# Unit 1's turns in the matmul banks, later clears on GpSimd, and the g product between the first turns of the keys

## The chip, the core and the metric

The kernel runs on one core of one Trainium2 chip. The metric is the device time of one execution, in microseconds (us). A core has a matrix engine, TensorE (PE in the profile, with its weight loads as PEld), three engines for everything else, VectorE (DVE), ScalarE (ACT) and GpSimd (POOL), and SyncE (SP), which issues DMAs only. GpSimd issues DMAs too: all loads from memory that change fp32 to fp16 on the way are issued by it, in the order of its program. Each engine works through its own instructions in order and waits where an operand is not ready.

TensorE writes to PSUM, a memory of eight banks that VectorE and ScalarE can read[...]. All other tiles are in SBUF.

## What is computed

Attention in chunks of 32 rows, then a layer norm, a two-layer network with a ReLU, and a residual:

```
for c in range(nc):                       # 24 chunks of 32 rows
    q_c = q[:, :, c_start:c_end]
    k_full = concat([mem_k, k[:, :, c_start - 16 : c_end + 8]], axis=2)   # 8 mem rows
    v_full = concat([mem_v, v[:, :, c_start - 16 : c_end + 8]], axis=2)
    a = softmax(scale * q_c @ k_full.T)
    attn[:, :, c_start:c_end] = a @ v_full
x  = attn as [4, 768, 512]                # 8 heads of 64
xn = (x - mean(x)) / sqrt(var(x) + 1e-6) * g_ln
out = x + max(xn @ w_ch1, 0) @ w_ch2      # 512 -> 2048 -> 512
```

There are 4 batches of 8 heads and 768 rows.

## The kernel before

Every engine's order is written out by hand: what the program calls first, the engine does first. A batch's 768 rows are 12 groups of 64 (two chunks); two groups make a tile of 128 rows, three tiles a unit. There are eight units, two per batch. The part that concerns us is the first two units, which are batch 0 and are interleaved by hand (lines 471 to 616); from unit 1's second half on, a plan of steps takes over (lines 619 to 717).

The steps of one tile, by function and line:

- `load_kq`, `load_v_group` (L105, L114): GpSimd loads keys, queries and values. The first 64 rows of `k16` and 48 of `q16` come first (`CUT`), in two halves of four heads; the rest later.
- `turn_kq` (L185): TensorE turns keys or queries of two heads (a "pair" j of four), 16 matmuls against the identity, into a PSUM bank. `keep_k` (L197) copies turned keys to `KT`, on VectorE unless told otherwise; `keep_q` (L210) copies turned queries to `QZ`, ScalarE or VectorE. `QZ` holds each query block beside a block of zeros, so that one matmul serves two heads; `clear_q` (L444) writes these zeros.
- `keep_mem` (L143) copies the 8 mem rows of the values into rows 96 to 103 of every group of `V`.
- `scores` (L293): 8 matmuls into an `att` buffer of two banks, then two exp on ScalarE into `AT`. `values` (L314): 16 matmuls into the next `att` buffer. `norm` (L326): VectorE divides (`xs`, L330), takes the mean (L336) and writes `xn` (L339), scaled by `g_row`, which is g_ln spread over all partitions by a product of a row of ones with g_ln (L492). `xs` is the last to read the `att` buffer.
- `turn_x` (L354): TensorE turns `xn` with four matmuls (L362), and ScalarE copies the result to `xT` (L367).
- `up` (L380): four matmuls (L387) into an `mm` bank and a ReLU on ScalarE (L393) or VectorE (L395). `hc` counts 16 blocks of 128 columns; block `hc` needs chunk `hc // 4` of `w1c`. `down` (L399) is the second layer.
- `stay_busy(n)` (L372): n matmuls on a tile of zeros whose result nobody reads. They fill time on TensorE.

PSUM has two `att` buffers of two banks and four `mm` banks, handed out in turn by `slot(kind)` (L86). A new user of a buffer waits for the last reader of the old one.

In the opening, TensorE runs eight fillers, the mem keys, and the g product; then the first turns of keys and queries for pairs 0 and 1, three fillers, keys of pairs 2 and 3, four fillers, and queries of pairs 2 and 3, which go into the banks that held the keys of pairs 0 and 1. GpSimd meanwhile issues loads (lines 509 to 526): values of groups 3 to 5, the first chunk of `w1c`, the remaining rows of keys and queries, the second chunk, values of groups 6 and 7, and so on to `w2c`. Tiles 0 to 2 need only groups 0 to 5; the second half of the queries and keys (groups 6 to 11) is turned in two `kq_block`s (L583), just ahead of which VectorE clears the later rows of `QZ` and copies the later mem rows (L579 to L581).

Of the kernel before, what the change touches and what calls it, by code (L numbers as in the profile page):

```python
# [15 lines left out]
def kernel(  # L16
# [12 lines left out]
    nc = tc.nc  # L29
# [3 lines left out]
    NG = 12  # L33
# [15 lines left out]
    g_row = sb.tile([128, 512], FP32, name="g_row")  # L49
    g_one = sb.tile([1, 512], FP32, name="g_one")  # L50
    ones32 = sb.tile([1, 128], FP32, name="ones32")
# [13 lines left out]
    QZ = [sb.tile([128, NG, 4, 2, 64], FP16, name=f"QZ{i}") for i in range(2)]  # L65
# [16 lines left out]
    att = [ps.tile([128, 2, 512], FP32, name=f"att{i}") for i in range(2)]  # L82
    mm = [ps.tile([128, 512], FP32, name=f"mm{i}") for i in range(4)]
    turn = {"att": 0, "mm": 0}

    def slot(kind):  # L86
        lst = {"att": att, "mm": mm}[kind]
        turn[kind] = (turn[kind] + 1) % len(lst)
        return lst[turn[kind]]

    def dram(t, offset, pattern):
        return bass.AP(tensor=t.tensor, offset=offset, ap=[list(p) for p in pattern])

    def free(ap, off, pattern, parts=None):

        p = list(ap.ap[0]) if parts is None else [ap.ap[0][0], parts]
        return bass.AP(tensor=ap.tensor, offset=ap.offset + off, ap=[p] + [list(x) for x in pattern])

    def as16(t):
        return t.bitcast(FP16)  # L100
# [4 lines left out]
    def load_kq(b, which, lo=0, hi=96, h0=0, h1=H):  # L105

        dst, src = ((k16, k), (q16, q))[which]
        nc.gpsimd.dma_start(
            out=dst[lo:hi, h0:h1, :, :],
            in_=dram(src, (b * H + h0) * HS + 512 * lo,  # L110
                     [[512, hi - lo], [HS, h1 - h0], [1, 512]]),
        )

    def load_v_group(b, g):  # L114

        lo, hi = max(64 * g - 16, 0), min(64 * g + 80, S)
        r = 16 + lo - 64 * g
        nc.gpsimd.dma_start(  # L118
            out=V[b % 2][r : r + hi - lo, g, :, 0:64],
            in_=dram(v, b * H * HS + lo * D, [[64, hi - lo], [HS, H], [1, 64]]),  # L120
        )
# [18 lines left out]
                        ap=[list(src.ap[0]), [0, NG], [1, H * HD]]),  # L140
        )

    def keep_mem(b, g0, g1):  # L143

        src = memv16[:, b, :, 0:64]
        nc.vector.tensor_copy(
            out=V[b % 2][96:104, g0:g1, :, 0:64],
            in_=bass.AP(tensor=src.tensor, offset=src.offset,
                        ap=[list(src.ap[0]), [0, g1 - g0], [HD, H], [1, 64]]),
        )  # L150

    def load_w1(c):
        nc.gpsimd.dma_start(
            out=w1c[c], in_=dram(moe_w_ch1, 512 * c, [[FF, 128], [128 * FF, 4], [1, 512]])
        )
# [8 lines left out]
    def mem_keys():  # L164

        pv = slot("mm")
        for i in range(2):
            for par in range(2):
                nc.tensor.matmul(
                    out=pv[64 * par : 64 * par + 64, 64 * i : 64 * i + 64],  # L170
                    lhsT=memk16[:, i, :],
                    rhs=free(identity, 8 * par, [[16, 8], [1, 8]]),
                    start=True, stop=True, tile_position=(0, 64 * par),
                )
        nc.vector.tensor_copy(out=memKT.rearrange("p j m -> p (j m)"), in_=pv[:, 0:128])

    def mem_cols(b):
        src = memKT[:, 4 * b : 4 * b + 4, :]
        nc.vector.tensor_copy(
            out=free(KT[b % 2], 96, [[KW, 4], [4 * KW, NG], [1, 8]]),  # L180
            in_=bass.AP(tensor=src.tensor, offset=src.offset,
                        ap=[list(src.ap[0]), [8, 4], [0, NG], [1, 8]]),
        )

    def turn_kq(pv, src, j, n):  # L185

        for r in range(8):
            for par in range(2):
                nc.tensor.matmul(  # L189
                    out=pv[64 * par : 64 * par + 64, n * r : n * r + n],  # L190
                    lhsT=src[0:n, 2 * j + par, r, :],
                    rhs=identity[0:n, 0:n],
                    is_transpose=True, start=True, stop=True,
                    tile_position=(0, 64 * par),
                )
# [158 lines left out]
    def turn_x(u, i, t, kind="att"):  # L354
        if kind == "dma":
            nc.sync.dma_start_transpose(
                out=xT[u % 2][:, :, 128 * i : 128 * i + 128], in_=xn[t % 3]
            )
            return
        pv = as16(slot("att")[:, 0, :]) if kind == "att" else as16(slot("mm")[:, :])  # L360
        for dt in range(4):
            nc.tensor.matmul(  # L362
                out=pv[:, 128 * dt : 128 * dt + 128],
                lhsT=xn[t % 3][:, 128 * dt : 128 * dt + 128], rhs=identity,
                is_transpose=True, start=True, stop=True,
            )
        nc.scalar.copy(  # L367
            out=xT[u % 2][:, :, 128 * i : 128 * i + 128],
            in_=free(pv, 0, [[128, 4], [1, 128]]),
        )  # L370

    def stay_busy(n, p=None):  # L372

        p = slot("mm") if p is None else p
        for _ in range(n):
            nc.tensor.matmul(out=p, lhsT=busy[:, 0:128], rhs=busy, start=True, stop=True)  # L376
# [59 lines left out]
    def clear_k(i):  # L436
        end = 4 * KW * NG
        nc.vector.memset(free(KT[i], 0, [[KW, 4], [1, 16]]), 0.0)
        nc.vector.memset(free(KT[i], 88, [[KW, 4 * NG], [1, 8]]), 0.0)
        nc.vector.memset(free(KT[i], 104, [[KW, 4 * NG], [1, 8]]), 0.0)  # L440
        nc.vector.memset(free(KT[i], end - 4 * KW + 80, [[KW, 4], [1, 8]]), 0.0)
        nc.vector.memset(KT[i][:, end : end + 32], 0.0)

    def clear_q(i, par, g0=0, g1=NG):  # L444

        nc.vector.memset(QZ[i][64 - 64 * par : 128 - 64 * par, g0:g1, :, par, :], 0.0)

    TWO_ONES = (2.0 ** -7) * (1 + 15 * 2.0 ** -13)

    def clear_v(i, eng, between=lambda: None, end=HD // 2):  # L450

        eng.memset(V[i][0:32, 0, :, 0:64], 0.0)
        eng.memset(V[i][64:96, NG - 1, :, 0:64], 0.0)
        eng.memset(V[i].bitcast(FP32)[:, :, :, 32:end], TWO_ONES)
        between()
        for c, g, rows in ((0, 0, slice(0, 32)), (1, NG - 1, slice(64, 96))):
            eng.tensor_copy(
                out=free(V[i][rows, g, 0, 64:65], 0, [[HD, H]]),
                in_=free(counts[rows, c : c + 1], 0, [[0, H]]),
            )  # L460
# [24 lines left out]
    nc.scalar.copy(out=memk16, in_=memk32)  # L485
    nc.scalar.copy(out=QZ[0][0:64, 0:6, :, 1, :], in_=free(busy[0:64, :], 0, [[0, 6], [0, 4], [1, 64]]))
    nc.scalar.copy(out=memv16[:, 0, :, 0:64], in_=memv32.rearrange("p (h d) -> p h d", h=H))
    stay_busy(8)
    clear_v(0, nc.vector, lambda: (clear_q(0, 0, 0, 6), clear_k(0)), 33)
    mem_keys()  # L490
    spare = att[turn["att"]]
    nc.tensor.matmul(out=spare[:, 1, :], lhsT=ones32, rhs=g_one, start=True, stop=True)  # L492
    nc.scalar.copy(out=g_row, in_=spare[:, 1, :])
    spare = spare[:, 0, :]
    mem_cols(0)
    for g in range(3):
        load_v_group(0, g)
# [14 lines left out]
    for which in range(2):  # L512
        load_kq(0, which, CUT[which], 96)
    load_w1(1)
    for g in range(6, 8):
        load_v_group(0, g)
    load_w1(2)
# [3 lines left out]
    for c in range(4):  # L521
        load_w2(c)
    nc.gpsimd.dma_start(
        out=memv16[:, 1:B, :, 0:64],
        in_=dram(mem_v, H * 512, [[64, 8], [512, (B - 1) * H], [1, 64]]),
    )

    vec, act = nc.vector.tensor_copy, nc.scalar.copy
    banks = [slot("mm")[:, :] for j in range(4)]
    first_k = [as16(p) for p in banks]  # L530
    first = slot("att")
    first_q = [as16(first[:, i, :]) for i in range(2)] + first_k[0:2]
    for j in range(2):
        turn_kq(first_k[j], k16, j, CUT[0])
    for j in range(2):
        turn_kq(first_q[j], q16, j, CUT[1])
    for j in range(2):
        keep_k(first_k[j], 0, j, CUT[0], 0, 7)
        for par in range(2):
            keep_q(act, first_q[j], 0, j, par, CUT[1], 0, 6)  # L540
    stay_busy(3, spare)
    for j in range(2, 4):
        turn_kq(first_k[j], k16, j, CUT[0])
    for j in range(2, 4):
        keep_k(first_k[j], 0, j, CUT[0], 0, 7, act if j == 2 else vec)
    stay_busy(4, spare)
    for j in range(2, 4):
        turn_kq(first_q[j], q16, j, CUT[1])
    for g0, g1 in ((0, 2), (2, 6)):
        for j in range(2, 4):  # L550
            for par in range(2):
                keep_q(act if j == 2 else vec, first_q[j], 0, j, par, CUT[1], g0, g1)
    keep_mem(0, 0, 6)
    scores(0, 0)
    scores(0, 1)
    stay_busy(3)
# [19 lines left out]
    turn_x(0, 2, 2)  # L576
    for hc in range(4):
        up(0, 3, hc, 2)
    for par in range(2):  # L579
        clear_q(0, par, 6, NG)  # L580
    keep_mem(0, 6, NG)  # L581
    stay_busy(2)
    for j in (0, 2):  # L583
        kq_block(0, j, 6, NG, "mm", vec if j else act)
        keep_rest()
# [11 lines left out]
    norm(4, 4)  # L597
    up(0, 3, 11)
    scores(0, 5)
    turn_x(1, 0, 3)  # L600
    for hc in range(4):
        up(1, 1, hc)
    values(0, 5)
    norm(5, 5)
    turn_x(1, 1, 4)
    for hc in range(4, 8):
        up(1, 1, hc)
    for hc in range(8):
        up(1, 2, hc, 1)
    for hc in range(8, 12):  # L610
        up(1, 2, hc)
    turn_x(1, 2, 5)
    for hc in range(12, 16):
        up(0, 3, hc)
    for hc in range(12):
# [4 lines left out]
    for u, tiles in list(enumerate(units))[1:]:  # L620
# [86 lines left out]
        for step in range(12 if u == 1 else 0, last + 1):  # L707
            if step < 16:
                up(u, n, step)
            else:  # L710
                i, part = divmod(step - 16, 4)
# [36 lines left out]
```

## Time and profile before

| | |
|---|---|
| median of 6 runs | 227.16 us (225.70 to 228.32) |
| the profiled execution | 225.70 us, of which the span from first to last instruction is 224.0 us |
| TensorE busy | 214.2 us, 96% of the span |
| TensorE's weight loads | 134.3 us, 60% |
| VectorE | 120.2 us, 54% |
| GpSimd | 105.3 us, 47% |
| ScalarE | 103.3 us, 46% |
| mean granted TensorE clock | 0.976 |

All durations come from the one profiled execution; it is the fastest of the six runs shown. The profile's page cuts the span into 40 slices of 5.6 us. A row of the timeline gives start, duration, engine, line, operation, what it writes and reads, how many instructions are merged, and in square brackets how long the engine was idle before it and what ended that. The four loads of `w1c` (512 KB each, counted as written) took 7.9 to 13.8 us from issue to landing, a group of `V` (96 KB) typically 5.8 us; all sixteen DMA engines were busy from 6 us to about 50 us.

### The profile page before, as it was taken

To read this page: it belongs to the slowest core of one execution; us is meant where nothing else is said; L and a number is where in the kernel's file an instruction comes from. 1 tells how busy PE (TensorE), PEld (TensorE's weight loads), DVE (VectorE), ACT (ScalarE), POOL (GpSimd) and SP (SyncE) were. 2 spreads that over 40 slices of the span, in tenths; PEclk is the share of its full clock that TensorE was granted. 3 is DMA by queue.
4 is the path that set the end of the run, shared out by engine and by line. 5 is a ranking of instruction groups with operands and counts; after the bars stand their busy time and mean duration, and the time that the engine had idled before them with its cause. 6 is when DMAs were issued, how large, how long until landed. Compare 5 with 4: busy or idle time off the path is not lost.

```text
span 224.0 us, 5194 instructions
## 1 busy us (share of the span) xinstructions
PE 214.2 (96%) x2071; PEld 134.3 (60%) x2071; DVE 120.2 (54%) x285; ACT 103.3 (46%) x216; POOL 105.3 (47%) x185
## 2 busy tenths in 40 slices
PE   7999986999999989999999999999999999999994
PEld 2566765986555557644775467546764576457553
DVE  5457768647763853951537446723375436634222
ACT  6567565457656467620275146501654055503200
POOL 7993554202899962996201599815229100210000
PEclk9769999699999999999999999999999999999999
DMA  5999999990299999997611399998655300421012
GB/s 87 162 151 194 181 192 214 203 169 3 41 160 178 179 187 190 97 152 200 108 26 40 83 188 159 141 152 147 115 146 142 120 0 4 94 70 47 3 47 94
DMA packets 87610, 27.25 MB, mean 122 GB/s; under 512 B 78289, under 2 KB 84081, under 8 KB 87538
## 3 DMA queue, kind: packets, MB, share of 16 engines
q0 software_dynamic: 62128, 14.38, 74.8%
q1 hardware_dynamic: 25458, 12.54, 25.0%
q8 instruction: 16, 0.26, 0.5%
q14 instruction: 8, 0.07, 0.1%
HBM read 28.84 MB, written 6.29 MB: 157 GB/s over the span
## 4 chain that ended last, share of the span: by engine, by line
PE 90%; DVE 7%; issue 1%; ACT 1%; DVEq 0%
PE mm L387 36%; PE mm L404 35%; PE att L299 4%; PE att L319 3%; PE mm L376 3%; PE att L189 2%; PE mm L422 2%; DVE KT L204 1%; PE mm L189 1%; DVE xs L330 1%; DVE xn L339 1%; PE att L376 1%; PE att L362 1%; ACT xT L367 1%; DVE rT L395 1%
## 5 line engine op out<-in xcount | busy, mean ns | idle before, releaser
L387 PE MATMUL mm<-xT,w1c 128*128 128x384 f16 (+2 forms) x624 | 91.3, 301 | 2.6 <-ACT xT L367 2.0
L404 PE MATMUL mm<-w2c,rT 128*128 128x512 f16 x338 | 76.3, 379 | 0.0
L387 PEld LDWEIGHTS <-w1c 128*128 128x128 f16 x624 | 61.8, 116 | 23.9 <-issue 3.1
L393 ACT ACTIVATE rT<-mm 128x384 f16<-128x384 f32 (+2 forms) x68 | 30.6, 454 | 71.4 <-PE mm L387 49.2
L404 PEld LDWEIGHTS <-rT 128*128 128x128 f16 x338 | 32.5, 98 | 36.9
L395 DVE TENSOR_SCALAR rT<-mm 128x384 f16<-128x384 f32 (+2 forms) x60 | 32.1, 540 | 36.4 <-PE mm L387 36.4
L411 DVE SCALAR_TENSOR_TENSOR osb<-mm,rstd,xs 128x512 f32<-128x512 f32 x23 | 17.3, 750 | 41.5 <-PE mm L404 31.1
L306 ACT ACTIVATE AT<-att,band 104x512 f16<-104x512 f32 x48 | 30.1, 685 | 11.8 <-PE att L299 11.6
L348 POOL TENSOR_SCALAR veps<-squares 128x1 f32<-128x1 f32 x24 | 4.7, 194 | 53.1 <-ACT junk L345 51.7
L118 POOL DMA_DIRECT2D V<-in_v_dram x24 | 18.8, 788 | 5.7 <-DVE rT L395 3.1
L345 ACT ACTIVATE junk<-xs,nmean 128x512 f16<-128x512 f32 x24 | 17.3, 720 | 7.3 <-DVE nmean L336 4.4
L339 DVE SCALAR_TENSOR_TENSOR xn<-xs,nmean,g_row 128x512 f16<-128x512 f32 x24 | 18.6, 776 | 0.8
L330 DVE SCALAR_TENSOR_TENSOR xs<-att,rec 128x512 f32<-128x512 f32 x24 | 16.6, 692 | 0.8
L299 PE MATMUL att<-QZ,KT 128*128 128x128 f16 x192 | 15.5, 226 | 1.1 <-DVE QZ L214 1.1
L287 POOL COPY QZ<-kraw 64x768 f16<-64x768 f16 x16 | 14.1, 884 | 4.5 <-DMA kraw<-qraw 4.0
L299 PEld LDWEIGHTS <-KT 128*128 128x128 f16 x192 | 13.2, 101 | 4.5 <-issue 1.3
L352 POOL TENSOR_TENSOR rstd<-veps,mhalf 128x1 f32<-128x1 f32 x24 | 13.6, 568 | 2.0
L279 POOL COPY KT<-KT 128x128 f16<-128x128 f16 (+4 forms) x16 | 4.2, 291 | 17.3 <-DMA KT<-kraw 17.2
L124 POOL DMA_DIRECT2D V<-in_v_dram x16 | 12.0, 771 | 0.5 <-PE mm L387 0.4
L319 PEld LDWEIGHTS <-AT 104*64 104x64 f16 x384 | 7.6, 111 | 6.4 <-issue 1.9
L252 POOL DMA_DIRECT2D kraw<-in_k_dram x12 | 11.2, 929 | 0.2 <-issue 0.2
L252 POOL DMA_DIRECT2D qraw<-in_q_dram x12 | 11.2, 933 | 0.0
(83 smaller groups left out, 158.2 us busy)
## 6 DMA issues: line engine op xcount, KB each, us to landing
out_dram<-osb SPq DMA_DIRECT2D x23, 256.0 KB, 2.4
V<-in_v_dram POOLq DMA_DIRECT2D x36, 96.0 KB, 5.8
w1c<-in_moe_w_ch_dram POOLq DMA_DIRECT2D x4, 512.0 KB, 10.6
w2c<-in_moe_w_ch_dram POOLq DMA_DIRECT2D x4, 512.0 KB, 11.8
kraw<-in_k_dram POOLq DMA_DIRECT2D x12, 128.0 KB, 5.9
qraw<-in_q_dram POOLq DMA_DIRECT2D x12, 128.0 KB, 5.9
qraw<-in_q_dram POOLq DMA_DIRECT2D x3, 384.0 KB, 14.6
kraw<-in_k_dram POOLq DMA_DIRECT2D x3, 256.0 KB, 4.4
```

What stands on the lines that cost most here:

```text
L118: nc.gpsimd.dma_start(out=V[b % 2][r : r + hi - lo, g, :, 0:64], in_=dram(v, b * H * HS + lo * D, [[64, hi - lo], [HS, H], [1, 64]]),)
L252: nc.gpsimd.dma_start(out=free(dst, 512 * t, [[64, H], [1, 64]]), in_=dram(src, b * H * HS + 128 * t * D, [[D, 128], [HS, H], [1, 64]]),)
L299: nc.tensor.matmul(out=p[:, gg, 128 * j : 128 * j + 128], lhsT=KT[b % 2][:, (4 * g + j) * KW : (4 * g + j) * KW + 128], rhs=QZ[b % 2][:, g ...
L306: nc.scalar.activation(out=free(a, 32 * c, [[512, 2], [64, 8], [1, 32]], KR), in_=free(p, 32 * c, [[512, 2], [64, 8], [1, 32]], KR), func= ...
L330: nc.vector.scalar_tensor_tensor(out=x.rearrange("p (h d) -> p h d", h=H), in0=free(p, 0, [[128, H], [1, 64]]), scalar=1.0, in1=free(r, 0, ...
L339: nc.vector.scalar_tensor_tensor(out=xn[i], in0=x, scalar=nmean[xi], in1=g_row, op0=ALU.add, op1=ALU.mult,)
L345: nc.scalar.activation(out=junk, in_=xs[xi], func=ACTF.Square, bias=nmean[xi], accum_out=squares[i],)
L387: nc.tensor.matmul(out=p, lhsT=free(w, i, [[4, 128]]), rhs=xT[u % 2][:, dt, lo:hi], start=(dt == 0), stop=(dt == 3),)
L393: nc.scalar.activation(out=o, in_=p, func=ACTF.Relu)
L395: nc.vector.tensor_scalar(out=o, in0=p, scalar1=0.0, scalar2=None, op0=ALU.max)
L404: nc.tensor.matmul(out=p, lhsT=rT[t // 3 == 1][hc][:, 128 * i : 128 * i + 128], rhs=w2c[hc // 4][:, hc % 4, :], start=(hc == 0), stop=(hc ...
L411: nc.vector.scalar_tensor_tensor(out=o, in0=p, scalar=rstd[t % 9], in1=xs[t % 9], op0=ALU.mult, op1=ALU.add,)
```

## The change

Three things change, with the fillers around them.

- The three `turn_x` of unit 1 (tiles 3 to 5) take an `mm` bank each in place of an `att` buffer.
- The clears of `QZ` for groups 6 to 11 (`clear_q(0, par, 6, NG)`, both halves) and the copy of the mem rows of these groups (`keep_mem(0, 6, NG)`) move from VectorE, just before the `kq_block`s, to GpSimd, where they stand between the load of the second chunk of `w1c` and the load of values of group 6. The two fillers after them are dropped. The copy of the mem rows of groups 0 to 5 stays on VectorE and moves up, from behind the queries of pairs 2 and 3 to behind the first keys.
- The g product, two passes over 512 columns ahead of the first turns and a copy on ScalarE, becomes two products of 256 columns between the first turns of the queries and the second turns of the keys. They go to the free halves of the two banks that hold the keys of pairs 0 and 1, and VectorE copies them to `g_row` after the last query copies. The fillers in the opening are now 10 (were 8), none (were 3) and 2 (were 4).

```diff
@@ -140,10 +140,10 @@
                         ap=[list(src.ap[0]), [0, NG], [1, H * HD]]),
         )
 
-    def keep_mem(b, g0, g1):
+    def keep_mem(b, g0, g1, copy):
 
         src = memv16[:, b, :, 0:64]
-        nc.vector.tensor_copy(
+        copy(
             out=V[b % 2][96:104, g0:g1, :, 0:64],
             in_=bass.AP(tensor=src.tensor, offset=src.offset,
                         ap=[list(src.ap[0]), [0, g1 - g0], [HD, H], [1, 64]]),
@@ -441,9 +441,9 @@
         nc.vector.memset(free(KT[i], end - 4 * KW + 80, [[KW, 4], [1, 8]]), 0.0)
         nc.vector.memset(KT[i][:, end : end + 32], 0.0)
 
-    def clear_q(i, par, g0=0, g1=NG):
-
-        nc.vector.memset(QZ[i][64 - 64 * par : 128 - 64 * par, g0:g1, :, par, :], 0.0)
+    def clear_q(i, par, g0=0, g1=NG, eng=nc.vector):
+
+        eng.memset(QZ[i][64 - 64 * par : 128 - 64 * par, g0:g1, :, par, :], 0.0)
 
     TWO_ONES = (2.0 ** -7) * (1 + 15 * 2.0 ** -13)
 
@@ -485,13 +485,9 @@
     nc.scalar.copy(out=memk16, in_=memk32)
     nc.scalar.copy(out=QZ[0][0:64, 0:6, :, 1, :], in_=free(busy[0:64, :], 0, [[0, 6], [0, 4], [1, 64]]))
     nc.scalar.copy(out=memv16[:, 0, :, 0:64], in_=memv32.rearrange("p (h d) -> p h d", h=H))
-    stay_busy(8)
+    stay_busy(10)
     clear_v(0, nc.vector, lambda: (clear_q(0, 0, 0, 6), clear_k(0)), 33)
     mem_keys()
-    spare = att[turn["att"]]
-    nc.tensor.matmul(out=spare[:, 1, :], lhsT=ones32, rhs=g_one, start=True, stop=True)
-    nc.scalar.copy(out=g_row, in_=spare[:, 1, :])
-    spare = spare[:, 0, :]
     mem_cols(0)
     for g in range(3):
         load_v_group(0, g)
@@ -512,6 +508,9 @@
     for which in range(2):
         load_kq(0, which, CUT[which], 96)
     load_w1(1)
+    for par in range(2):
+        clear_q(0, par, 6, NG, nc.gpsimd)
+    keep_mem(0, 6, NG, nc.gpsimd.tensor_copy)
     for g in range(6, 8):
         load_v_group(0, g)
     load_w1(2)
@@ -530,6 +529,7 @@
     first_k = [as16(p) for p in banks]
     first = slot("att")
     first_q = [as16(first[:, i, :]) for i in range(2)] + first_k[0:2]
+    spare = att[(turn["att"] + 1) % 2][:, 0, :]
     for j in range(2):
         turn_kq(first_k[j], k16, j, CUT[0])
     for j in range(2):
@@ -538,19 +538,26 @@
         keep_k(first_k[j], 0, j, CUT[0], 0, 7)
         for par in range(2):
             keep_q(act, first_q[j], 0, j, par, CUT[1], 0, 6)
-    stay_busy(3, spare)
+    keep_mem(0, 0, 6, vec)
+
+    for i in range(2):
+        nc.tensor.matmul(
+            out=banks[i][:, 256:512], lhsT=ones32, rhs=g_one[:, 256 * i : 256 * i + 256],
+            start=True, stop=True,
+        )
     for j in range(2, 4):
         turn_kq(first_k[j], k16, j, CUT[0])
     for j in range(2, 4):
         keep_k(first_k[j], 0, j, CUT[0], 0, 7, act if j == 2 else vec)
-    stay_busy(4, spare)
+    stay_busy(2, spare)
     for j in range(2, 4):
         turn_kq(first_q[j], q16, j, CUT[1])
     for g0, g1 in ((0, 2), (2, 6)):
         for j in range(2, 4):
             for par in range(2):
                 keep_q(act if j == 2 else vec, first_q[j], 0, j, par, CUT[1], g0, g1)
-    keep_mem(0, 0, 6)
+    for i in range(2):
+        vec(out=g_row[:, 256 * i : 256 * i + 256], in_=banks[i][:, 256:512])
     scores(0, 0)
     scores(0, 1)
     stay_busy(3)
@@ -576,10 +583,6 @@
     turn_x(0, 2, 2)
     for hc in range(4):
         up(0, 3, hc, 2)
-    for par in range(2):
-        clear_q(0, par, 6, NG)
-    keep_mem(0, 6, NG)
-    stay_busy(2)
     for j in (0, 2):
         kq_block(0, j, 6, NG, "mm", vec if j else act)
         keep_rest()
@@ -597,19 +600,19 @@
     norm(4, 4)
     up(0, 3, 11)
     scores(0, 5)
-    turn_x(1, 0, 3)
+    turn_x(1, 0, 3, "mm")
     for hc in range(4):
         up(1, 1, hc)
     values(0, 5)
     norm(5, 5)
-    turn_x(1, 1, 4)
+    turn_x(1, 1, 4, "mm")
     for hc in range(4, 8):
         up(1, 1, hc)
     for hc in range(8):
         up(1, 2, hc, 1)
     for hc in range(8, 12):
         up(1, 2, hc)
-    turn_x(1, 2, 5)
+    turn_x(1, 2, 5, "mm")
     for hc in range(12, 16):
         up(0, 3, hc)
     for hc in range(12):
```

## What I expect, before the run

> **What bounds the kernel now.** I read the page first: the engine shares of the chain that ended last, and the clock row.
>
> ```profile
> PEclk9769999699999999999999999999999999999999
> ...
> PE 90%; DVE 7%; issue 1%; ACT 1%; DVEq 0%
> ```
>
> TensorE is the bound (busy 96% of 224.0 us), so only its idle time, its filler matmuls and its clock can be gained. The clock row dips in slices of 5.6 us: the second, the third and the eighth. All that the change touches starts before 47 us, so next I read TensorE's waits in the first 60 us (us in total, times, longest).
>
> ```profile
> PE mm L387 <- ACT xT L367: 1.3, 2, 0.7
> ...
> PE att L299 <- DVE QZ L214: 1.1, 2, 0.8
> PE att L362 <- DVE xs L330: 1.0, 1, 1.0
> ```
>
> The last two are what this change bears on. Their place is in TensorE's timeline (start, duration, line, count, idle before):
>
> ```profile
> 22.84 1.05 PE L387 MATMUL mm<-xT,w1c 128*128 128x128 f16 x16 [0.67 <-ACT xT L367]
> 23.74 0.59 PE L376 MATMUL mm<-busy 128*128 128x512 f16 x2
> 24.26 0.87 PE L189 MATMUL att<-identity,kraw 96*64 96x96 f16 x32
> ...
> 27.11 2.19 PE L387 MATMUL mm<-xT,w1c 128*128 128x384 f16 x12
> 29.13 0.33 PE L299 MATMUL att<-QZ,KT 128*128 128x128 f16 x3
> 30.29 0.44 PE L299 MATMUL att<-QZ,KT 128*128 128x128 f16 x5 [0.82 <-DVE QZ L214]
> ...
> 36.89 0.38 PE L362 MATMUL att<-identity,xn 128*128 128x128 f16 x4 [1.03 <-DVE xs L330]
> 37.95 1.05 PE L387 MATMUL mm<-xT,w1c 128*128 128x128 f16 x16 [0.67 <-ACT xT L367]
> ```
>
> At 29.46 the scores stop for 0.82 us, because VectorE has not copied the last queries. Why VectorE is late stands in its own timeline:
>
> ```profile
> 24.22 0.70 DVE L446 MEMSET QZ<- 64x768 uint32 x1 [0.22 <-issue]
> 25.11 0.70 DVE L446 MEMSET QZ<- 64x768 uint32 x1 [0.20 <-issue]
> 25.83 0.96 DVE L146 COPY V<-memv 8x3072 f16<-8x3072 f16 x1
> 26.80 2.41 DVE L204 COPY KT<-att 128x352 f16<-128x352 f16 x8
> ```
>
> It clears and copies mem rows until 26.79, though the first turned keys are there at about 24.7. Its queue then runs without a hole to the last query copy at 30.24.
>
> **Part by part.** Sums are made against the profiled execution (225.7 us, span 224.0). It was the fastest of the six; the median is 1.46 us above it.
>
> *Clears and mem rows to GpSimd, fill before the key turns gone.* The chain of waits gives the two fillers 0.43 us beyond what overlaps (23.90 to 24.33); with the issue around them the turns start 0.4 to 0.59 us earlier. VectorE drops 2 x 0.70 + 0.96 us and begins copying keys at about 24.3. Its remaining work (26.80 to 30.24, 3.44 us) then follows the turns, which last 2.85 us: it ends at about 28.0. ScalarE's six query copies (25.51 to 28.43) move up with the turns, so the bank of each "up" is free when it was. Turns 23.90 to 26.75, three "up" 2.0 us, scores from 28.5 to 29.15, against an end at 30.73 before: 1.4 to 1.6 us, taken as 1.5. What is late next is TensorE itself, and w1c chunk 2 at about 30.1.
>
> *What that puts on GpSimd.* GpSimd's memset of 32x512 fp16 took 0.54 us and of 128x768 0.74 us, 0.84 to 0.96 ns per element: 1536 elements are 1.4 us each. Its copies of 128x64 to 128x256 took 0.23 to 0.40 us, 0.84 ns per element over 0.18: 3072 elements are 2.8 us. Together 5.6 us, put in front of the V loads of groups 6 to 11, w1c 2 and 3, all of w2c, memv and the next batch's keys.
>
> ```profile
> 13.51 1.95 POOL L118 DMA_DIRECT2D V<-in_v_dram  x2
> ...
> 18.95 0.77 POOL L118 DMA_DIRECT2D V<-in_v_dram  x1 [1.95 <-DMA w1c<-in_moe_w_ch_dram]
> ```
>
> The loads of groups 6 and 7 then go out at about 19.1 to 20.7. I cost that at nothing, since the transfers run in order behind a backlog: GpSimd's waits end when w1c 0 lands at 18.95, w1c 1 at 25.80 and w1c 2 at 29.56. The last 3.76 us fit groups 6, 7 and w1c 2 (96+96+512 KB at 190 GB/s, 3.7 us), so nothing issued at 13.5 moved before 25.8. GpSimd has 6 us to spare there; without that cover w1c 2 would land 5 us late, at 35, with TensorE waiting.
>
> *The g product.* Out: two passes of 1.05 us on the chain ahead of the first turns, and ScalarE's copy (0.58). In: two fillers there, and two half products after the first query turns, in place of three fillers (0.75) and with two of the later four gone. The keys' weight load waited 0.76 us for its DMA until 6.08, so the first turns do not move. The first half starts at 7.4; the second shares a bank with keys that VectorE reads until 8.16 and may have to wait. Then, with the clock at half from 8.44: second keys end at 9.9, two fillers 10.8, queries 11.85, against 11.80. From -0.6 (no wait) to +0.5; I take 0. A gain would be capped at 0.2: w1c 0 lands at 18.95 and its first matmul runs at 19.14. VectorE's two copies to g_row (0.43 each, from the 128x256 row of L395 at 425 ns) fall between its query copies (13.3) and norm at 15.81, which also holds if the fillers after the scores must wait for their banks (to about 14.2, with the scores ending at 14.05). mem rows 0 to 5 move to VectorE's hole from 8.16 to 9.03: they take 0.98, so the keys behind them may start 0.1 late, which the fillers hide.
>
> *Unit 1's turns in matmul banks.* The wait of 1.03 for xs goes, but ScalarE's queue takes its place: exp of the last scores runs 35.95 to 37.21 and stands ahead of the xT copy (37.31 before). The next "up" starts at 37.85 in place of 37.95: 0.1 us. With one bank fewer the later "up"s could lose up to 0.2; VectorE's norm to 41.39 stalls them anyway. I take 0.1 gained.
>
> Sum: 0 + 1.5 + 0.1 = 1.6 us on 225.7. From this fast run to the median I carry 1.4.
>
> **A rule against the removed filler.** Stretches of 3.41 us, as the clock changes cut them (duration, then busy us and instructions of PE, PEld, DVE, ACT, POOL, then granted clock):
>
> ```profile
> 5.02:8.44 3.42, 3.42 (x93) 2.00 (x91) 2.16 (x6) 1.56 (x4) 3.22 (x12) 1.00 1.22 188
> ...
> 22.09:25.50 3.41, 2.74 (x78) 2.23 (x77) 1.66 (x4) 1.26 (x4) 0.72 (x1) 1.00 1.56 189
> ...
> 35.74:39.15 3.41, 1.71 (x37) 1.40 (x36) 2.56 (x8) 2.44 (x6) 1.72 (x3) 1.00 1.05 209
> 39.15:42.57 3.42, 3.38 (x44) 3.05 (x38) 2.40 (x8) 1.31 (x4) 1.16 (x3) 0.50 1.16 203
> ```
>
> The first has TensorE busy throughout, with 1.64 us of turns and the g product in it, and half clock follows. The third has 1.05 us of "up", and half clock follows. The second has the same 1.05 us of "up", 0.59 of filler and 1.24 of turns, and the clock held. The Trainium skill (TensorE: Matmul & The Clock Gate, Part 4) says that transposes do not count as busy in the same way. By that rule the second stretch keeps 1.05 us without its filler and the turns and "up"s from 25.5 run at half clock. By the trace it still has more turns than the third. The sum is -1.6 or, worked out below, about +1.5.
>
> **Rivals.** *The shared port* (slower). GpSimd's mem copy would run from 16.3 to 19.1, in the middle of the norms (xn at 16.98, 18.81, 20.64). The trace shows GpSimd and VectorE disturbing each other: a GpSimd copy of 64x768 took 1.33 us beside an xn against 0.825 alone, and one xn took 1.31 us against 0.752 beside a GpSimd DMA issue. The Trainium skill (SBUF — State Buffer, section "SBUF: two separate sides") says that whoever starts first holds the pair for its whole instruction against a VectorE operation with two SBUF inputs. Then xn waits until 19.1, 2.1 us, and everything to 22.84 moves with it: -1.6 + 2.1 = +0.5, 227.6. Against it: an xn at 96.24 started 0.1 us before a GpSimd copy ended and still took 0.75. The point from which it decides is 1.6 us of blocking. With the trace's 0.56 us per meeting it costs about 0.5.
>
> *The clock falls at the turns.* Half clock from 25.5 adds 0.6 us to the turns and leaves the "up"s to run at half until 28.9; if that stretch does not warm it either (it was 8.44 to 15.26 in one piece before), scores end at 32.3, 1.6 us later than now: 228.7. Against it: in other executions the stretches fall elsewhere, and before also holds 2.85 us of bare turns.
>
> *It also clears the dip at 39.15.* With the gap of 35.9 to 37.95 moved 1.5 us up, no stretch is as empty; at full clock TensorE would gain 0.4 to 0.7 after 41.73: 225.0.
>
> *A load decides after all* (5.6 us on GpSimd become 11): 230.
>
> **How the numbers follow.** 227.16 - 1.4 = 225.8. Cases: relief as summed 0.40 (own range 224.8 to 226.8); relief and no dip 0.18; port 0.20; clock 0.17; late load 0.05. Within 1% is 224.9 to 229.4, about what a measurement of this kernel can tell from no change. Faster: a quarter of the first and somewhat over half of the second, 0.2. Slower: half of the clock case, a fifth of the port, most of the last, 0.16. The range 224.2 to 229.0 leaves out the ends of the second and fourth and the last.
>
> **What would show it.** Right: no wait of scores on QZ near 29; VectorE's key copies from about 24.3; xT copy straight behind the exp near 36; groups 6 and 7 landing as before. Wrong: an xn of 2 us and more between 16 and 20 beside the GpSimd copy; granted clock 0.5 between 25 and 32; TensorE waiting for w1c near 30; a GpSimd copy far from 2.8 us.

## The result, and the profile after

| | before | after |
|---|---|---|
| median | 226.98 us (72 runs) | 225.78 us (35 runs) |
| ratio of the times, 95% interval | | 0.9948 [0.9929, 0.9968] |
| profiled execution, span | 225.70 us, 224.0 us | 224.76 us, 223.1 us |

The change makes the kernel 1.2 us faster, about half a per cent. Medians here and below are of all executions; ratios and intervals leave out those more than 1.5% above the fastest of the same kernel.

TensorE's waits in the first 60 us of the changed kernel (us in total, times, longest) show that the gain is not the one that was summed:

```profile
PE mm L387 <- ACT xT L367: 2.3, 2, 1.7
...
PE att L362 <- DVE xn L339: 0.9, 1, 0.9
PE mm L387 <- DVE kraw L395: 0.8, 1, 0.8
...
PE att L299 <- DVE QZ L214: 0.2, 1, 0.2
```

The waits for QZ near 29 us and for xs are gone. ScalarE's xT copy has taken the place of the second, and a wait for xn, which barely existed before, is new. TensorE's timeline after:

```profile
20.85 0.40 PE L362 MATMUL att<-identity,xn 128*128 128x128 f16 x4 [0.94 <-DVE xn L339]
...
23.87 1.05 PE L387 MATMUL mm<-xT,w1c 128*128 128x128 f16 x16 [0.67 <-ACT xT L367]
24.86 0.87 PE L189 MATMUL att<-identity,kraw 96*64 96x96 f16 x32
...
29.73 0.61 PE L299 MATMUL att<-QZ,KT 128*128 128x128 f16 x8
...
35.31 0.39 PE L362 MATMUL mm<-identity,xn 128*128 128x128 f16 x4
37.35 1.05 PE L387 MATMUL mm<-xT,w1c 128*128 128x128 f16 x16 [1.66 <-ACT xT L367]
```

The "up" that stood at 22.84 is at 23.87: 1.03 us lost. From there to the end of tile 3's scores the kernel took 7.89 us before (22.84 to 30.73) and takes 6.47 (23.87 to 30.34): 1.42 gained. From the start of tile 5's scores to the next "up" it took 2.70 (35.25 to 37.95) and takes 2.49 (34.86 to 37.35): 0.21 gained. The sum is 0.60, which is what 37.95 against 37.35 shows. Another 0.53 comes later: the half clock from 39.15 to 42.57 did not occur in this execution, and `down` begins at 52.70 (53.83 before), although a wait of 0.83 us for VectorE at 41.00 is new. Of these 1.13 us the time of the profiled execution shows 0.94.

Where the 1.03 went stands in VectorE's timeline and GpSimd's:

```profile
8.07 0.96 DVE L146 COPY V<-memv 8x3072 f16<-8x3072 f16 x1
...
16.89 0.75 DVE L339 SCALAR_TENSOR_TENSOR xn<-xs,nmean,g_row 128x512 f16<-128x512 f32 x1
...
18.71 2.08 DVE L339 SCALAR_TENSOR_TENSOR xn<-xs,nmean,g_row 128x512 f16<-128x512 f32 x1
```

```profile
8.08 0.99 POOL L503 TENSOR_TENSOR zero<-zero 128x1 f32<-128x1 f32 x1
...
11.61 0.79 POOL L153 DMA_DIRECT2D w1c<-in_moe_w_ch_dram  x1
...
14.40 2.80 POOL L446 MEMSET QZ<- 64x1536 f16 x2
17.26 2.98 POOL L146 COPY V<-memv 8x3072 f16<-8x3072 f16 x1
20.19 1.55 POOL L118 DMA_DIRECT2D V<-in_v_dram  x2
```

The second xn begins while GpSimd copies mem rows and takes 2.08 us in place of 0.75. It ends at 20.79, 0.55 after the copy. The same pair of engines meets the other way round at 8 us: VectorE's copy of mem rows 0 to 5 (8.07 to 9.03) stretches an operation of GpSimd on one column from 0.19 to 0.99 us, and every load behind it goes out 0.8 us later than in the kernel before:

```profile
8.07 0.19 POOL L507 TENSOR_TENSOR zero<-zero 128x1 f32<-128x1 f32 x1
...
10.79 0.79 POOL L153 DMA_DIRECT2D w1c<-in_moe_w_ch_dram  x1
```

Without these 0.8 us GpSimd's mem copy would have begun near 16.4, ahead of the first xn (16.89), and would have met that one (an estimate from the two timelines).

### The profile page after: what moved, and what is told of

It is laid out like the page before. It is cut to its first block, busy times and chain, and to the rows that moved or that the text cites. A ratio compares the mean times of both kernels' runs of the same rounds, so it can differ in the third digit from the quotient of the medians.

```text
span 223.1 us, 5197 instructions
## 1 busy us (share of the span) xinstructions
PE 212.2 (95%) x2068; PEld 133.1 (60%) x2068; DVE 120.3 (54%) x284; ACT 102.4 (46%) x215; POOL 110.2 (49%) x188
## 4 chain that ended last, share of the span: by engine, by line
PE 78%; DMA 9%; DVE 6%; SPq 2%; issue 2%; ACT 1%; POOL 1%; DVEq 0%; POOLq 0%
PE mm L387 32%; PE mm L404 31%; PE att L299 4%; DMA V<-V 4%; PE att L319 3%; DMA KT<-kraw 3%; PE att L189 2%; DMA qraw<-in_q_dram 2%; DVE xn L339 2%; DVE xs L330 2%; PE mm L422 2%; PE mm L189 1%; PE mm L376 1%; ACT xT L367 1%; PE att L362 1%
## 5 line engine op out<-in xcount | busy, mean ns | idle before, releaser
L387 PE MATMUL mm<-xT,w1c 128*128 128x384 f16 (+2 forms) x624 | 90.2, 298 | 3.9 <-ACT xT L367 3.0
L387 PEld LDWEIGHTS <-w1c 128*128 128x128 f16 x624 | 60.7, 114 | 25.2 <-issue 4.5
L339 DVE SCALAR_TENSOR_TENSOR xn<-xs,nmean,g_row 128x512 f16<-128x512 f32 x24 | 20.1, 839 | 0.9
L118 POOL DMA_DIRECT2D V<-in_v_dram x24 | 18.3, 772 | 0.1
L279 POOL COPY KT<-KT 128x128 f16<-128x128 f16 (+4 forms) x16 | 4.2, 290 | 17.6 <-DMA KT<-kraw 17.5
L124 POOL DMA_DIRECT2D V<-in_v_dram x16 | 12.0, 806 | 0.2 <-issue 0.2
L214 ACT COPY QZ<-att 64x768 f16<-64x768 f16 (+1 forms) x12 | 8.2, 686 | 6.9 <-PE att L189 6.7
```

What stands on the lines that cost most here:

```text
L118: nc.gpsimd.dma_start(out=V[b % 2][r : r + hi - lo, g, :, 0:64], in_=dram(v, b * H * HS + lo * D, [[64, hi - lo], [HS, H], [1, 64]]),)
L339: nc.vector.scalar_tensor_tensor(out=xn[i], in0=x, scalar=nmean[xi], in1=g_row, op0=ALU.add, op1=ALU.mult,)
L387: nc.tensor.matmul(out=p, lhsT=free(w, i, [[4, 128]]), rhs=xT[u % 2][:, dt, lo:hi], start=(dt == 0), stop=(dt == 3),)
```

## The experiments

The theory after the result: the relief of VectorE works as summed (1.42 us), and the copy on GpSimd takes 1.03 us of that back by holding xn. The rivals: the long xn has another cause; the fillers held the clock; the gain came from the turns or from the opening. Ratios are to the kernel before, timed together with each experiment. Its median moved between 226.42 and 227.06 us from one set of runs to another, so experiments are compared by ratio and not by median.

**E1 to E3: the copy elsewhere.**

```diff
 # e1: behind value group 10
-    keep_mem(0, 6, NG, nc.gpsimd.tensor_copy)
...
     for g in range(8, NG):
+        if g == NG - 1:
+            keep_mem(0, 6, NG, nc.gpsimd.tensor_copy)
         load_v_group(0, g)
 # e2: ahead of the clears
+    keep_mem(0, 6, NG, nc.gpsimd.tensor_copy)
     for par in range(2):
         clear_q(0, par, 6, NG, nc.gpsimd)
-    keep_mem(0, 6, NG, nc.gpsimd.tensor_copy)
 # e3: on VectorE, ahead of the second turns
-    keep_mem(0, 6, NG, nc.gpsimd.tensor_copy)
...
+    keep_mem(0, 6, NG, vec)
     for j in (0, 2):
         kq_block(0, j, 6, NG, "mm", vec if j else act)
```

> As the changed kernel, but GpSimd's copy of the later mem rows stands between the loads of value groups 10 and 11 (about 22 us), behind the norms of tiles 0 to 2. If that copy holds VectorE's xn (2.08 us in place of 0.75 in the changed kernel): every xn before 22 us takes 0.75, the key turns begin at about 23.9 (24.86 in the changed kernel), the scores of tile 3 end near 29.3 (30.34), and the median is about 1.0 us below the changed kernel's 225.78. If the long xn comes from something else there (the memsets, the DMA issues): it stays near 2 us and the time stays at 225.8.

> As the changed kernel, but GpSimd does the mem copy ahead of the two memsets. If only an operation that reads SBUF on GpSimd holds xn: the copy ends near 17.3, the first xn (due at 16.9) waits 0.4 and the others take 0.75 beside the memsets; key turns near 24.3, some 0.6 us below the changed kernel. If a memset holds it too: the second xn (due near 19) waits until a memset ends, up to 1.3 us, and the time is that of the changed kernel or worse.

> As the changed kernel, but the later mem rows are copied by VectorE again, just ahead of the second turns; the clears stay on GpSimd. Port theory: every xn takes 0.75, the key copies begin about 0.7 later than in e1 (near 24.9) and are done before the scores need them (28.6 against 28.6), so within 0.2 us of e1, 0.8 to 1.0 below the changed kernel. If the relief of VectorE by the mem copy were what the change lives on: slower than the changed kernel by up to 1.0.

Measured: 224.48, 224.37 and 224.62 us, ratios 0.9930 [0.9903, 0.9957], 0.9921 [0.9888, 0.9954] and 0.9945 [0.9920, 0.9971]. In all three every xn before 23 us takes 0.75, so the long xn goes with the copy. The gain in time is less clear: by ratio the three lie 0.4, 0.6 and 0.1 us below the changed kernel, and all three intervals overlap its own. The 0.8 to 1.0 us that E1 and E3 were expected to gain on it were not measured; the profiled executions of E2 and E3 show 0.7 and 0.8 (`down` at 52.02 and 51.94, against 52.70). E2 shows which of GpSimd's operations holds it; its GpSimd timeline, and VectorE's:

```profile
14.33 2.74 POOL L146 COPY V<-memv 8x3072 f16<-8x3072 f16 x1
17.13 2.78 POOL L446 MEMSET QZ<- 64x1536 f16 x2
```

```profile
18.78 0.75 DVE L339 SCALAR_TENSOR_TENSOR xn<-xs,nmean,g_row 128x512 f16<-128x512 f32 x1
```

An xn in the middle of the memsets is not held. So it is the copy, which reads SBUF, and not work on GpSimd as such. The second turns begin at 24.17 in E2 and 24.09 in E3 (24.86 in the changed kernel), not at the 23.9 that E1's expectation gave: a wait for w1c chunk 0 (0.30 and 0.20 us, near 19.4) has come up, which E10 takes up. E1's profiled execution had its opening at half clock (the first 32 turns in 1.06 us against 0.69, although the recorded clock reads 1.00 there), with its first xn at 18.29 in place of 16.9, so its start times cannot be compared; the length of its xn can. That E3 is no worse also shows that VectorE did not need relief from the copy, only from the clears.

**E4 and E8: the fillers.** The two fillers back in the changed kernel, and taken out of the kernel before:

```diff
 # e4
+    stay_busy(2)
     for j in (0, 2):
         kq_block(0, j, 6, NG, "mm", vec if j else act)
 # e8, in the kernel before
     keep_mem(0, 6, NG)
-    stay_busy(2)
     for j in (0, 2):
```

> As the changed kernel, with the two fillers ahead of the second turns again. If a filler is only time: 0.4 to 0.6 us slower in the median. If it holds the clock in those executions whose 3.41 us stretches fall badly: no slower in the median, with fewer times near 227, perhaps 0.3 faster.

> The kernel before without the two fillers ahead of the second turns. If VectorE's queue sets the scores there: turns 0.5 earlier, scores end where they did (30.7), ratio 1.000. If the fillers hold the clock: up to 1.005, more executions near 228. If fillers are plain time: 0.998.

E4: 225.43 us, 0.9974 [0.9950, 0.9998]; E8: 226.45 us, 1.0012 [0.9988, 1.0037]. E4 points to a filler that is only time (0.26% above the changed kernel's ratio), but the two intervals overlap. Its timeline agrees: from "up" to turns takes 1.42 us there (25.46 to 26.88) and 0.99 in the changed kernel, so the fillers cost 0.43 where nothing waits. It also shows that the hold changes from execution to execution: half clock in its opening lasted until 17.6 us, and so the copy on GpSimd (17.05 to 19.79) met the first xn, at 17.55, and lengthened it by 2.04 us to 2.79. E8 is the other half: its turns do start 0.43 sooner after the "up", but the wait of the scores for VectorE grows from 0.82 to 1.26 us, and nothing is gained. The fillers cost nothing here while VectorE is later than they are. What speaks most plainly on the clock is E7, the kernel before with the middle part alone; one stretch of 3.41 us between two possible changes of its clock, and the next (columns as in the prediction):

```profile
24.64:28.05 3.41, 3.41 (x133) 3.20 (x133) 2.50 (x9) 2.41 (x6) 2.44 (x4) 1.00 1.53 160
28.05:31.47 3.42, 3.42 (x33) 2.60 (x32) 2.20 (x5) 2.50 (x6) 1.06 (x2) 1.00 1.71 177
```

Of the first stretch 2.86 us are turns and 0.64 "up", with no filler, and the clock stays whole. The "up" alone would not explain that: the stretch from 35.74 in the prediction had 1.05 us of "up", and half clock followed it. In the ten profiles without the filler (the changed kernel, E1 to E3, E7 to E12) no clock below 1 is recorded between 23 and 35 us.

**E5 to E7: one part of the change each, on the kernel before.** The diffs are the three parts of the change.

> The kernel before with unit 1's turns in matmul banks and nothing else. If ScalarE's queue takes the place of the wait: the turn near 36 no longer waits, the next up begins 2.5 us after the last scores began (2.70 before), 0.1 to 0.3 us gained, a ratio of 0.999. If the wait of 1.03 is gained whole: 0.9955.

> The kernel before with the opening alone changed (fillers, g product, mem rows of groups 0 to 5 earlier). If the early mem copy on VectorE holds GpSimd up near 8 us (a one-column operation took 0.99 us there in the changed kernel against 0.19) and so w1c chunk 0: its issue near 11.6, first up 0.2 to 0.4 us late, ratio 1.001. If the opening is neutral as forecast: 1.000, first up near 19.1.

> The kernel before with only the later clears and mem rows on GpSimd and without the two fillers. GpSimd is not held up in the opening here, so its copy begins near 16.4, ahead of the first xn (16.98). Port theory: that xn lasts until about 19.7, the key turns begin near 26, and 2.1 us lost outweigh 1.5 gained: ratio 1.000 to 1.003. If no more is lost than in the changed kernel (1.03): 0.998.

E5, the turns: 225.78 us, 0.9979 [0.9953, 1.0006]. The expected mechanism is there: the turn no longer waits, and 2.49 us lie between tile 5's scores and the "up" (35.46 to 37.95). 0.2 us by the trace; the time itself is not clear of no change. E6, the opening: 226.23 us, 0.9987 [0.9964, 1.0010], no change that can be told. One operation of GpSimd near 8.4 took 0.83 and w1c chunk 0 went out at 11.46, but the profiled opening ran at half clock (its first 32 turns, too, took 1.06 us), so the first "up" can't be compared. E7, the middle: 226.32 us, 0.9998 [0.9970, 1.0026]. It lies at the lower edge of the first expectation, but its interval holds the second too. The copy did not begin at 16.4: VectorE's other mem copy, at its old place near 13.5, stretched GpSimd's two clears from 2.80 to 3.56 us, and the copy, from 17.24 to 19.98, met the second xn:

```profile
18.06 2.47 DVE L339 SCALAR_TENSOR_TENSOR xn<-xs,nmean,g_row 128x512 f16<-128x512 f32 x1
```

So the part of the change that was to bring almost everything brings nothing on its own that can be told; the hold of xn, 1.72 us here, stands against its relief. By their times none of the three parts is clear of no change, so the times do not say which of them brings the half per cent. That it is the relief is read from the timelines.

**E9: the copy twice.**

```diff
     keep_mem(0, 6, NG, nc.gpsimd.tensor_copy)
+    keep_mem(0, 6, NG, nc.gpsimd.tensor_copy)
```

> As the changed kernel, with GpSimd's copy of the later mem rows issued twice in a row (the second writes the same values again), 17.3 to about 23.1. If each GpSimd copy holds xn to its own end and VectorE gets the port between two of them: two xn of 1.5 to 2.9 us, each ending about 0.6 after a copy, and the key turns some 1.5 to 2.3 us later than the changed kernel's 24.86. If only one xn can be held, or the hold is a fixed time: one xn near 2.1 and the turns at 24.9.

One run, so its time says little: 230.65 us. The copies on GpSimd, and VectorE's xn:

```profile
17.07 5.90 POOL L146 COPY V<-memv 8x3072 f16<-8x3072 f16 x2
```

```profile
17.55 2.81 DVE L339 SCALAR_TENSOR_TENSOR xn<-xs,nmean,g_row 128x512 f16<-128x512 f32 x1
21.43 2.08 DVE L339 SCALAR_TENSOR_TENSOR xn<-xs,nmean,g_row 128x512 f16<-128x512 f32 x1
```

Each copy holds one xn, and the second ends 0.54 us after the last copy (22.97). The turns begin at 27.57, 2.7 us later than in the changed kernel and 0.4 more than the upper end expected. Of these, 0.66 us come from the opening, where half clock lasted longer (first xn at 17.55 against 16.89); the other 2.05 are within what was expected, and match the longer holding of xn (3.39 us in place of 1.33). The two copies together took 0.4 us more than twice 2.74, as they would if the first xn ran between them.

**E10 and E11: neither collision.** The mem rows of groups 0 to 5 go to ScalarE, on top of E3 and E2.

```diff
     nc.scalar.copy(out=memv16[:, 0, :, 0:64], in_=memv32.rearrange("p (h d) -> p h d", h=H))
+    keep_mem(0, 0, 6, nc.scalar.copy)
...
-    keep_mem(0, 0, 6, vec)
```

> As e3 (later mem rows on VectorE, clears on GpSimd), and the mem rows of groups 0 to 5 copied by ScalarE in its idle time near 5 us. If VectorE's early copy is what held GpSimd up at 8 us: no operation of GpSimd there above 0.3 us, w1c chunk 0 issued near 10.8 in place of 11.6, the first up near 19.0 with no wait for w1c, and 0.2 to 0.4 us less than e3 (ratio about 0.991). If not: issue at 11.6 and the time of e3. ScalarE's copy should take 2.9 us by its 0.613 for 512 columns and 1.47 for 1536, to about 8, and delay its first query copies by 0.5 without effect on the scores.

> As e2 (GpSimd copies the later mem rows ahead of the clears), and the mem rows of groups 0 to 5 on ScalarE. The GpSimd copy then runs 13.5 to 16.3, before the first xn near 16.9. Port theory: no xn over 0.8 before 22 us, the first up near 19.0, 0.2 to 0.4 us less than e2 and within 0.2 us of e10 (ratio about 0.991).

E10: 224.0 us, 0.9855 [0.9804, 0.9906]; E11: 224.16 us, 0.9867 [0.9811, 0.9922]. GpSimd's timeline in E10:

```profile
8.07 0.19 POOL L504 TENSOR_TENSOR zero<-zero 128x1 f32<-128x1 f32 x1
...
10.79 0.79 POOL L153 DMA_DIRECT2D w1c<-in_moe_w_ch_dram  x1
```

With VectorE's copy away, nothing holds GpSimd there; w1c goes out 0.8 us sooner and the first "up" runs at 19.07 with no wait for it (19.40 in E3). The second turns begin at 23.76 and 23.75. ScalarE's copy took 2.75 us (5.04 to 7.79) and cost nothing visible. So VectorE's copy is what held GpSimd. What that costs in time is not shown: the turns are 0.33 us sooner than in E3, but from issue to landing this load took 7.8 us in E3, 6.6 in E10, 8.1 in E11, and only 7.0 in the changed kernel, where it went out as late as in E3 and nothing waited for it. By ratio E10 lies 0.9% below E3 (intervals apart) and E11 0.5% below E2 (intervals overlap), about 2.0 and 1.2 us and more than the 0.2 to 0.4 expected; what brings the rest is open.

**E12: ScalarE's order.** On top of E10, the turn ahead of the last scores:

```diff
+    turn_x(1, 0, 3, "mm")
     scores(0, 5)
-    turn_x(1, 0, 3, "mm")
```

> As e10, with unit 1's first turn ahead of the scores of tile 5, on TensorE and so on ScalarE too (xT copy ahead of the exp). If ScalarE's order is what took the place of the wait for xs: TensorE's wait of 1.66 for xT shrinks to about 0.5, values of tile 5 come some 0.9 earlier, and 0.6 to 0.9 us less than e10's 224.0 (ratio 0.982 to 0.984). If the turn then waits for xn as long as it saves, or the norm of tile 5 sets what follows: within 0.2 us of e10.

Measured: 223.3 us, 0.9839 [0.9779, 0.9899]. The wait for xT near 35 shrinks from 1.66 to 0.23:

```profile
35.08 1.05 PE L387 MATMUL mm<-xT,w1c 128*128 128x128 f16 x16 [0.23 <-ACT xT L367]
```

`down` begins at 50.63 (51.61 in E10): 1.0 us in the first stage, so ScalarE's order was what had replaced the wait for xs. In the profiled execution, the slowest of the six, it was given back at 162.7 us:

```profile
162.74 0.70 PE L319 MATMUL att<-V,AT 104*64 104x65 f16 x32 [1.88 <-DMA V<-V]
```

The copies of value rows between groups for batch 3 landed later than TensorE came. The changed kernel shows the same wait with 0.50 us, E11 with 0.81, E10 none. What sets their landing was not tried. E12's time is not clear of E10's: their intervals overlap almost whole. E10 to E12 all beat the kernel before and, by their intervals, the changed kernel: moving both copies out of the way is a gain clear of noise, while what each collision costs by itself is known from single timelines only.

## Why the prediction was right, and where its sum was not

The forecast was 225.8 us and 1.4 us gained; measured are 225.78 and 1.2. It was right in what the change does, but that the time agrees so closely is in part luck. In the profiled execution the terms of its sum come to 0.60 us (1.42 + 0.21 - 1.03) in place of 1.6; another 0.53 came from a dip of the clock that the sum had not counted on. The median it started from, of six executions, was also 0.18 us higher than that of 72.

- *Relief of VectorE:* forecast 1.4 to 1.6, measured 1.42 in the timelines. The scores' wait on QZ is gone, the key copies follow the turns. E8 confirms that VectorE and not the filler set the scores before.
- *Fillers as plain time:* right, on the path 0.43 us (E4).
- *Durations on GpSimd:* forecast 1.4 per clear and 2.8 for the copy; measured 1.40 and 2.74 where nothing disturbs them. The loads stayed behind the backlog: w1c chunk 2 landed at 28.56, before at 29.56, and the values of groups 6 and 7 took 4.7 us from issue to landing where they had taken 12.4.
- *Turns in matmul banks:* forecast 0.1, measured 0.21. ScalarE's queue took the place of the wait, as stated.
- *The step that was mis-sized* is "what that puts on GpSimd", which the sum cost at nothing because the loads are hidden. They are, but the port is not: 1.03 us at the "up". The prediction had this as a rival with chance 0.20, at 2.1 us if the copy met the first xn. In the changed kernel's profile it met the second, since the opening had moved GpSimd by 0.8 us: 1.33 us of holding, below the 1.6 us from which it would have decided. In E4's it did meet the first, with 2.04. The first of its signs of being wrong, an xn of 2 us and more between 16 and 20, did occur (2.08 us at 18.71). Its evidence against the rival could not tell: the xn at 96.24 began 0.1 us before a copy ended, and since a held xn here ends 0.54 us after the copy, one that begins in the copy's last 0.2 us takes no longer than its own 0.75 (an estimate from these figures).
- *The opening:* forecast 0 for TensorE, and so it is (first "up" at 19.05, 19.14 before). What was not seen is that the move of mem rows 0 to 5 holds GpSimd up at 8 us. Its price is open: in the changed kernel's profile no wait for w1c follows from it.
- *The dip at 39.15:* not in this execution, 0.53 us, which the sum gave to another case. In the profile it makes up for half of the port. The four profiles with the old opening (before, E5, E7, E8) have half clock somewhere between 38 and 44 us, the ten with the new opening have none there. Whether the opening keeps it away, or where the stretches happen to fall, was not tried. (The case was put at 225.0; 225.8 less the 0.4 to 0.7 is 225.1 to 225.4.)
- *The clock at the turns:* the rival with chance 0.17 did not occur in any profile, not even in E7's, where nearly a whole stretch was turns.

Two rules were weighed. The Trainium skill (SBUF — State Buffer, "SBUF: two separate sides") says that whichever operation starts first holds the pair of ports that VectorE and GpSimd share for its whole length, and that a VectorE operation with two SBUF inputs meets only a GpSimd operation that reads SBUF; the held xn (0.54 to 0.55 us beyond the copy's end) and E2's (0.75 us beside the memsets) agree with both. The Trainium skill (TensorE: Matmul & The Clock Gate, Part 4) says that transposes do not count as busy in the same way; for these turns of 96 rows E7 shows otherwise (2.86 us of turns in 3.41, clock 1.00 after it), and the measurement decides.

## What to carry to other kernels

Work moved to an idle engine has to be checked for what it shares with the busy one, not only for its place in its queue: here a long copy on GpSimd, off every chain, lengthened VectorE's operation with two SBUF inputs. Place such a copy where VectorE has no such operation (E1, E2, E11), or leave it on VectorE where that has room (E3); ScalarE took the other mem copy without a visible cost (E10). When a wait goes, ask whose queue is next in order behind it: in one profiled execution each, moving the turn ahead of the scores gained 1.0 us in the first stage, and freeing its bank 0.21.

## What the runs showed of the hardware

- GpSimd's 8x3072 copy holds VectorE's two-input xn to its end: in four executions the held xn ended 0.54 to 0.55 us after the copy (after, E4, E7, E9). Two clears of 64x1536 by memset do not hold it (E2).
- The reverse: VectorE's 0.96 us fp16 copy from SBUF to SBUF held GpSimd's one-column operation for 0.8 us (after), and its two memsets for 0.76 (E7).
- The recorded clock changes only at multiples of 3.41 us from one another, and turns of 96 rows kept it whole (2.86 of 3.41 us, E7); in the opening of the kernel before, a stretch with 1.64 us of turns of 48 and 64 rows and the g product in it was followed by half clock. What tells the two apart was not tried.
